# A segment's attention scores as one product over 128 key columns, in attention followed by two feed-forward layers

## The chip, the cores and the metric

One core of one Trainium2 chip runs the whole program. The time is device microseconds of one execution; smaller is better.

## The reference

Three layers in a row, on 4 batches of 544 tokens (32 global, 512 local) and 512 features:

```python
# attention, 8 heads of 64, window 32, scale 1/8
s_g  = scale * q_g @ concat(k_g, k_l).T           # a global query sees all 544 keys
out_g = sm(s_g) @ concat(v_g, v_l)
s_ll = where(abs(i - j) <= 32, scale * q_l @ k_l.T, -1e9)
s_lg = scale * q_l @ k_g.T                        # a local query: its window and the 32 globals
out_l = sm(concat(s_lg, s_ll)) @ concat(v_g, v_l)
x = concat(out_g, out_l)                          # rows of tokens, 512 wide
# feed forward, 512 -> 2048 -> 512
x = (relu(x @ w_in) ** 2) @ w_out
# routed experts: tokens with x @ w_skip > 0 go to one of 8 experts, the others pass
out = x + gate * (relu(x @ w1[e]) @ w2[e])
```

`sm` is the softmax over the last axis. All inputs are float32 values, those of w_in and w_out lie 8 bytes apart and are rebuilt on the chip.

## The kernel before

**Tiles and segments.** The 512 local queries of a batch are 4 tiles of 128, so there are 16 tiles t (batch t // 4, place tt = t % 4 in it). A tile has 4 segments of 32 queries, and each segment sees 96 local keys (a window of three blocks of 32, moved inward at the ends of the sequence) and 32 global keys. The scores of a tile are two PSUM banks `sc` of 128 queries x 4 heads x 128 columns: columns 0 to 95 are the window, 96 to 127 the global keys.

**Scores (`attention`, L413).** `kT[b]` holds the keys of a batch, transposed: 128 partitions (two heads of 64) x 4 pairs of heads x 544 columns, the 512 local keys first and the 32 global ones behind. For a pair of heads the loop writes first the windows of the 4 segments for both heads, then the global columns: 16 products for a pair, 64 for a tile. Each uses 64 rows and 32 columns of TensorE (PE):

```python
for p in range(NPAIR):
    for globals_ in (False, True):
        for i in range(NQ):
            w0 = window(tt, i)
            keys, cols = (slice(SL, S), slice(WIN, P)) if globals_ else (slice(w0, w0 + WIN), slice(0, WIN))
            for g in range(2):
                rows = slice(D * g, D * (g + 1))
                nc.tensor.matmul(scs[g][SEG*i:SEG*(i+1), p, cols], lhsT=q[rows, p, SEG*i:SEG*(i+1)], rhs=kT[b][rows, p, keys], ...)
```

**The rest of a tile.** VectorE (DVE) adds the mask (L426, three masks: first tile of a batch, middle, last), takes the maximum (L430) and scales it (L431). ScalarE (ACT) computes the exps (L433). PE transposes them (L442), ACT or DVE copies them out (L444), and PE multiplies with the values (L451, 32 products into `po`). The value rows of a window stand on 128 partitions in the order of the score columns: rows 0 to 95 the window (L369, L377), rows 96 to 127 the global values (L370, L380). Tiles 0 and 1 use seven places that nothing else uses (`st_v`), the later ones six places in turn (`vr`).

**Keys.** `prep_globals` (L316 to L324) and `prep_k` (L326 to L331) transpose keys on PE into the two-buffered PSUM tag "tr" and copy them to `kT[b]` with ACT: L320 (the globals, 128 columns) and L331 (512 columns, four times for a batch).

**Global queries (`attention_global`).** L485: four products over 512 keys (`gsa`) and four over 32 (`gsb`) for each half of the heads, eight such blocks in all.

**Feed forward and experts.** While the attention of a tile runs, PE works through the feed-forward products of the tiles before it: L697 and L723 at the start, where weights still come in, L700 to L702 and L725 to L727 later. Each chunk of weights is loaded by SP (L209), rebuilt by ACT (L219) and DVE (L223, L227, L233). The activation of the hidden layer runs on ACT (L704, L743) and DVE (L741). Experts follow from some 480 us on.

**Order.** The order of all this is written by hand in strings of letters (SEQ for the first five tiles, EVEN, ODD, TAIL), which a driver turns into calls. Each engine does its instructions in program order, and waits at each for what it needs. SP issues nearly all loads, in order.

Of the kernel before, what the change touches and what calls it, by code (L numbers as in the profile page):

```python
# [8 lines left out]
F32 = mybir.dt.float32  # L9
# [45 lines left out]
def attention_ffn_routed_experts(  # L55
# [73 lines left out]

    masks = {}  # L130
    for kind in range(3):
        m = const.tile([P, P], F32, name=f"mask{kind}")
        nc.gpsimd.memset(m, 0.0)
        for i in range(NQ):
            shift = 0
            if kind == 0 and i == 0:
                shift = SEG
            if kind == 2 and i == NQ - 1:
                shift = -SEG
            seg = m[SEG * i:SEG * (i + 1), 0:WIN]  # L140
            nc.gpsimd.affine_select(
                out=seg, in_=seg, compare_op=ALU.is_ge, fill=NEG,
                base=shift, pattern=[[1, WIN]], channel_multiplier=-1,
            )
            nc.gpsimd.affine_select(
                out=seg, in_=seg, compare_op=ALU.is_ge, fill=NEG,
                base=2 * SEG - shift, pattern=[[-1, WIN]], channel_multiplier=1,
            )
        masks[kind] = m
# [195 lines left out]
    def window(tt, i):  # L345
        return min(max(tt * P + i * SEG - SEG, 0), SL - WIN)

    vin, vgl = {}, {}
    windows, opening, opening_places = [], [], []
# [3 lines left out]
    def load_v(t, part):  # L353
        if t >= NLT:
            return
        b, tt = divmod(t, TPB)
        for i in range(2 * part, 2 * part + 2):
            w0 = window(tt, i)
            if i and w0 == window(tt, i - 1):
# [17 lines left out]
            nc.sync.dma_start(heads(windows[k][0:WIN]), v_l[b, :, w0:w0 + WIN, :].rearrange("h s d -> s h d"))  # L377
            if globals_in.get(k) != b:
                globals_in[k] = b
                nc.sync.dma_start(heads(windows[k][WIN:P]), v_g[b].rearrange("h s d -> s h d"))  # L380
            assert all(w is not windows[k] for w in vin.values())
            vin[t, i] = windows[k]
# [9 lines left out]
    def attention(t, S_TAG, O_TAG):  # L392
        b, tt = divmod(t, TPB)
        q = qT[t // 2][:, :, (t % 2) * P:(t % 2 + 1) * P]
        mask = masks[0 if tt == 0 else 2 if tt == TPB - 1 else 1]
# [10 lines left out]
        for p in range(NPAIR):  # L406
            for globals_ in (False, True):
                for i in range(NQ):
                    w0 = window(tt, i)
                    keys, cols = (slice(SL, S), slice(WIN, P)) if globals_ else (slice(w0, w0 + WIN), slice(0, WIN))  # L410
                    for g in range(2):
                        rows = slice(D * g, D * (g + 1))
                        nc.tensor.matmul(  # L413
                            scs[g][SEG * i:SEG * (i + 1), p, cols],
                            lhsT=q[rows, p, SEG * i:SEG * (i + 1)], rhs=kT[b][rows, p, keys],
                            start=True, stop=True,
                        )
# [4 lines left out]
        for g in range(2):  # L422
            if t != 1:
                sms[g] = sb("sm", 2, [P, S], f"sm{t}_{g}")[:, 0:4 * P]
# [53 lines left out]
    def attention_global(b, S_TAG, O_TAG):  # L478
        for g in range(2):
            sa = ps.tile([P, SL], F32, tag=S_TAG, bufs=BANKS[S_TAG], name=f"gsa{b}_{g}")  # L480
            sb_ = pair(f"gsb{b}_{g}")[:, 0, 0:SG]
            for o, c, n in ((sa, 0, SL), (sb_, SL, SG)):
                for hh in range(4):
                    p, r = divmod(4 * g + hh, 2)
                    nc.tensor.matmul(  # L485
                        o[SG * hh:SG * (hh + 1), :],
                        lhsT=qgT[b][D * r:D * (r + 1), p, :], rhs=kT[b][D * r:D * (r + 1), p, c:c + n],
                        start=True, stop=True,
                    )
# [5 lines left out]
            pg = sb("sm", 2, [P, S], f"pg{b}_{g}")  # L495
            rs = sb("osum", 2, [P, H], f"grs{b}_{g}")
            nc.scalar.activation(pg[:, 0:SL], sa, AF.Exp, bias=mx[:, 3:4], scale=SCALE, accum_out=rs[:, 0:1])
            nc.scalar.activation(pg[:, SL:S], sb_, AF.Exp, bias=mx[:, 3:4], scale=SCALE, accum_out=rs[:, 1:2])
# [5 lines left out]
            for c in range(TPB):  # L504
                nc.tensor.transpose(ptr[:, c, :], pg[:, 0:SL].rearrange("p (k j) -> p j k", j=TPB)[:, c], ident)
# [3 lines left out]
            nc.tensor.transpose(ptr[0:SG, 0, :], pg[:, SL:S], ident)  # L509
# [245 lines left out]
    def ffn_tile(t):  # L755
# [3 lines left out]
        place = sb("kT", 1, [P, NPAIR, S], f"g{t}").rearrange("p a s -> p (a s)")  # L759
# [181 lines left out]
    def wide_tile(e):  # L941
# [4 lines left out]
        def first(f):  # L946
# [8 lines left out]
            gl = sb("sm", 2, [P, S], f"ewgl_{e}_{f}")[:, 0:WIDE].bitcast(F32R)  # L955
# [23 lines left out]
        ys = sb("kT", 1, [P, NPAIR, S], f"ewys_{e}").rearrange("p a s -> p (a s)")[:, 0:KD * WIDE]  # L979
# [42 lines left out]
    def expert_tile(e, j, si):  # L1022
# [4 lines left out]
        hl = sb("kT", 1, [P, NPAIR, S], f"ehl_{name}").rearrange("p a s -> p (a s)")[:, 0:2 * KE * P].bitcast(F32R)  # L1027
# [8 lines left out]
        def first(fb, k0, k1):  # L1036
# [8 lines left out]
            if k1 == KD:  # L1045
                rs[fb] = sb("sm", 2, [P, S], f"er_{name}_{fb}")[:, 0:512]
                nc.scalar.activation(rs[fb], h, AF.Relu)
# [118 lines left out]
    def rest_tile(e, j, in_arm, o):  # L1166
# [13 lines left out]
        r = sb("sm", 2, [P, S], f"er_rest{e}")[:, 0:fw]  # L1180
# [31 lines left out]
    with tc.manual_schedule():  # L1212
# [48 lines left out]
        idle = sb("sm", 2, [P, S], "idle").bitcast(BF16)[:, 0:DM]  # L1261
# [50 lines left out]
        both = sb("kg", 1, [P, 2 * NSLOT], "slots", I32)  # L1312
# [96 lines left out]
        def more(e, j):  # L1409

            if j == UNROLL:
                with tc.For_i(UNROLL, (n_tok[e] + (P - 1)) // P, 1) as it:
                    gi = sb("gi", 2, [P, 1], f"gi{e}", I32)
# [190 lines left out]
```

## Time and profile before

| | |
|---|---|
| median of 3 runs | 708.66 us (707.76 to 709.51) |
| the profiled execution | 710.78 us |
| its span, first to last instruction | 709.1 us, mean granted TensorE clock 0.980 |
| PE busy | 683.5 us, 96% |
| weight loads on PE (PEld) | 574.3 us |
| DVE busy | 396.2 us, 56% |
| ACT busy | 365.5 us, 52% |
| GpSimd (POOL) busy | 163.7 us, 23% |
| DMA | 93.90 MB in 118758 packets, 84789 of them under 512 B |

Times are counted from the span's start. A matmul in float32 leaves two records in the trace for each product. Records overlap on PE, so the sum of their lengths is longer than the time they take; the pace is read from the start of one group to the start of the next. "<-" behind an idle time names what ended it; "issue" means nothing that the profile shows. PEclk is the granted clock, 1.00 being 2.4 GHz and 0.50 being 1.2 GHz.

### The profile page before, as it was taken

Reading aid. Unit: us, or ns where it says so; the run is one execution under the profiler, and the core shown is the slowest. Engines: PE = TensorE matmul, PEld = TensorE weight load, DVE = VectorE, ACT = ScalarE, POOL = GpSimd, SP = SyncE. Lnnn points to the kernel's source line nnn. Section 1 sums busy time; section 2 is a strip of 40 time slices with the busy share of each in tenths; the row PEclk is TensorE's granted clock in tenths of the full one; section 3 lists DMA queues with packets and bytes.
Section 4 is the critical chain, followed back from the end, with each engine's and each line's share of the span. In section 5 each row is a group of like instructions: output and inputs, shape, how many; then the busy total and the mean of one; then the engine's idle time right before and its main releaser. Section 6 shows DMA issues by size and latency. Waiting matters only on the chain. (4 is left out here: it accounts for less than half of the span.)

```text
span 709.1 us, 18592 instructions
## 1 busy us (share of the span) xinstructions
PE 683.5 (96%) x7621; PEld 574.3 (81%) x7621; DVE 396.2 (56%) x1073; ACT 365.5 (52%) x939; POOL 163.7 (23%) x205
## 2 busy tenths in 40 slices
PE   6789999999999999999999999999999999999996
PEld 4566668788888888988898888888887887898875
DVE  1879973873556166165516526544338733915984
ACT  5756557665535545453555545344434514515862
POOL 6000043354211121211221221122220432401311
PEclk8699999999999999999999999999999999999998
DMA  9999744056052501306350120410026588962920
GB/s 273 245 276 245 281 112 106 2 130 125 2 139 61 146 31 36 84 2 146 91 109 32 36 75 2 161 62 1 31 84 201 204 272 285 374 254 77 388 96 21
DMA packets 118758, 93.90 MB, mean 132 GB/s; under 512 B 84789, under 2 KB 91957, under 8 KB 118660
## 3 DMA queue, kind: packets, MB, share of 16 engines
q1 hardware_dynamic: 108352, 71.01, 35.9%
q10 hardware_dynamic: 8292, 15.48, 6.6%
q0 software_dynamic: 2016, 6.09, 2.5%
q8 instruction: 63, 1.03, 0.6%
q14 instruction: 35, 0.29, 0.1%
HBM read 80.31 MB, written 12.66 MB: 131 GB/s over the span
## 5 line engine op out<-in xcount | busy, mean ns | idle before, releaser
L184 POOL TENSOR_TENSOR gl<-g,gh 128x256 fp32r<-128x256 f32 x107 | 79.7, 745 | 302.8 <-ACT gh L183 142.3
L700 PE MATMUL h<-xh,w_in 128*128 128x256 f32 x464 | 134.9, 291 | 0.7 <-ACT xh L183 0.7
L701 PE MATMUL h<-xl,w_in 128*128 128x256 f32 x464 | 129.6, 279 | 0.3 <-DVE xl L184 0.3
L702 PE MATMUL h<-xh,w_in 128*128 128x256 f32 x464 | 129.7, 280 | 0.0
L725 PE MATMUL acc<-w_out,gh 128*128 128x512 f32 x232 | 97.5, 420 | 1.5 <-ACT gh L183 1.5
L727 PE MATMUL acc<-w_out,gl 128*128 128x512 f32 x232 | 91.9, 396 | 0.2
L726 PE MATMUL acc<-w_out,gh 128*128 128x512 f32 x232 | 91.6, 395 | 0.0
L700 PEld LDWEIGHTS h<-xh,w_in 128*128 128x128 f32 x464 | 87.1, 188 | 4.2 <-ACT xh L183 0.9
L704 ACT ACTIVATE g<-h 128x256 f32<-128x256 f32 x128 | 48.9, 382 | 78.9 <-PE h L702 45.0
L701 PEld LDWEIGHTS h<-xl,w_in 128*128 128x128 f32 x464 | 87.2, 188 | 2.6 <-DVE xl L184 0.5
L702 PEld LDWEIGHTS h<-xh,w_in 128*128 128x128 f32 x464 | 87.1, 188 | 0.1
L433 ACT ACTIVATE sm<-sm,mx 128x128 f32<-128x128 f32 x120 | 46.7, 390 | 48.3 <-DVE mx L431 48.3
L741 DVE TENSOR_TENSOR g<-h,g 128x256 f32<-128x256 f32 x53 | 22.2, 420 | 85.5 <-ACT g L704 85.4
L183 ACT CAST gh<-g 128x256 fp32r<-128x256 f32 x116 | 47.2, 407 | 42.4 <-DVE g L741 40.1
L727 PEld LDWEIGHTS acc<-w_out,gl 128*128 128x128 f32 x232 | 43.5, 188 | 11.9 <-POOL gl L184 1.5
L725 PEld LDWEIGHTS acc<-w_out,gh 128*128 128x128 f32 x232 | 43.6, 188 | 8.6 <-ACT gh L183 1.9
L726 PEld LDWEIGHTS acc<-w_out,gh 128*128 128x128 f32 x232 | 43.8, 189 | 5.7
L426 DVE TENSOR_TENSOR sm<-sc,mask 128x512 f32<-128x512 f32 x30 | 20.6, 688 | 24.5 <-PE sc L413 23.7
L255 POOL TENSOR_TENSOR w_in<-st_raw_in,w_in 128x512 fp32r<-128x512 f32 x10 | 13.0, 1309 | 83.1 <-ACT w_in L251 83.1
L743 ACT ACTIVATE g<-g 128x256 f32<-128x256 f32 x63 | 26.2, 416 | 5.1 <-ACT g L704 2.6
L413 PEld LDWEIGHTS sc<-kT,qT 64*32 64x32 f32 x2048 | 25.0, 109 | 4.3 <-issue 3.5
L413 PE MATMUL sc<-kT,qT 64*32 64x96 f32 (+1 forms) x2048 | 27.1, 229 | 0.1
(634 smaller groups left out, 1466.5 us busy)
## 6 DMA issues: line engine op xcount, KB each, us to landing
st_e<-in_moe_w_dram SPq DMA_DIRECT2D x46, 512.0 KB, 5.6
vr<-in_v_l_dram SPq DMA_DIRECT2D x49, 192.0 KB, 4.1
st_raw_in<-in_moe_w_in_dram SPq DMA_DIRECT2D x16, 512.0 KB, 8.1
st_raw_out<-in_moe_w_out_dram SPq DMA_DIRECT2D x16, 512.0 KB, 8.0
st_e<-in_moe_w_dram ACTq DMA_DIRECT2D x12, 512.0 KB, 5.3
x2d<-x ACTq DMA_DIRECT2D x19, 256.5 KB, 3.8
st_gv<-in_v_l_dram SPq DMA_DIRECT2D x8, 512.0 KB, 5.5
out_dram<-x ACTq DMA_DIRECT2D x16, 256.0 KB, 3.7
```

The costliest lines, as they stand in the source:

```text
L183: nc.scalar.copy(hi, src)
L184: (lo_engine or nc.vector).tensor_tensor(out=lo, in0=src, in1=hi.bitcast(F32), op=ALU.subtract)
L413: nc.tensor.matmul(scs[g][SEG * i:SEG * (i + 1), p, cols], lhsT=q[rows, p, SEG * i:SEG * (i + 1)], rhs=kT[b][rows, p, keys], start=True, s ...
L433: nc.scalar.activation(sm[:, hh, :], sm[:, hh, :], AF.Exp, bias=mx[:, hh:hh + 1], scale=SCALE, accum_out=osum[:, 2 * hh + g:2 * hh + g + 1],)
L700: nc.tensor.matmul(h, lhsT=wh, rhs=xh[:, k, :], start=(k == 0), stop=False)
L701: nc.tensor.matmul(h, lhsT=wh, rhs=xl[:, k, :], start=False, stop=False)
L702: nc.tensor.matmul(h, lhsT=wl, rhs=xh[:, k, :], start=False, stop=(k == KD - 1))
L704: nc.scalar.activation(g, h, AF.Relu)
L725: nc.tensor.matmul(acc[z], lhsT=gh[:, c], rhs=wh, start=first_one, stop=False)
L726: nc.tensor.matmul(acc[z], lhsT=gh[:, c], rhs=wl, start=False, stop=False)
L727: nc.tensor.matmul(acc[z], lhsT=gl[:, c], rhs=wh, start=False, stop=last_one)
L743: nc.scalar.activation(square, g, AF.Square)
```

## The change

The keys of a batch are laid out so that every window has the global keys beside it. `kT[b]` gets 21 blocks of 32 columns: the 16 blocks of local keys, with a copy of the 32 global keys behind each group of three (five copies). Any three local blocks in a row and the copy between or behind them are then 128 columns that lie together, and a segment's scores are one product of 128 columns: 32 products for a tile. In the middle of the order of columns (and of value rows) the globals stand at 96, 64 or 32 by the window's place modulo 3 (`globals_at`).

- Keys: `prep_globals` copies the globals to five places at once, `prep_k` copies 480 columns and then 32. For batch 0 the copy of the globals and that of the last 32 columns are on DVE, else on ACT.
- Masks: one for each tt, four instead of three, in bfloat16, of 32x32 pieces.
- Values: a window whose globals stand within it is loaded in two DMAs. Of the seven windows of tiles 0 and 1 only the first gets its global values by DMA; GpSimd copies them into the other six (L399 of the changed kernel).
- `attention_global`: the product over 512 keys becomes one over five runs of 96 and one over 32.
- Some tiles get other sizes or other places for that (not shown): `kT` is larger, `sm` smaller, the expert lists lie in the masks' tile.

```diff
+    BLOCKS = SL // SEG
+    KEYS = (BLOCKS + (BLOCKS - 1) // 3) * SEG
+    def place(n):
+        return (n + n // 3) * SEG
+    def first_block(tt, i):
+        return min(max(tt * NQ + i - 1, 0), BLOCKS - 3)
+    def globals_at(w):
+        return (3 - w % 3) * SEG
...
     def prep_globals(b):
-        kT[b] = sb("kT", 1, [P, NPAIR, S], f"kT{b}")
+        kT[b] = sb("kT", 1, [P, NPAIR, KEYS], f"kT{b}")
         tr = pair(f"kgtr{b}")
         transposes(tr, kin[b, "g"][:, 0:DM], SG)
-        nc.scalar.copy(kT[b][:, :, SL:S], tr[:, :, 0:SG])
+        put = nc.vector.tensor_copy if b == 0 else nc.scalar.copy
+        put(
+            kT[b][:, :, 0:KEYS - SEG].rearrange("p a (g c) -> p a g c", c=P)[:, :, :, WIN:P],
+            tr[:, :, 0:SG].unsqueeze(2).to_broadcast([P, NPAIR, KEYS // P, SG]),
+        )
...
-        nc.scalar.copy(kT[b][:, p, 0:SL].rearrange("p (q j) -> p j q", j=TPB), tr)
+        q = WIN * (KEYS // P) // TPB
+        nc.scalar.copy(
+            kT[b][:, p, 0:KEYS - SEG].rearrange("p (g q j) -> p j g q", j=TPB, q=P // TPB)[:, :, :, 0:WIN // TPB],
+            tr[:, :, 0:q].rearrange("p j (g q) -> p j g q", q=WIN // TPB),
+        )
+        put = nc.vector.tensor_copy if b == 0 else nc.scalar.copy
+        put(kT[b][:, p, KEYS - SEG:KEYS].rearrange("p (q j) -> p j q", j=TPB), tr[:, :, q:P])
...
+    def load_window(o, b, w):
+        at = globals_at(w)
+        for row, n, key in ((0, at, w * SEG), (at + SG, WIN - at, w * SEG + at)):
+            if n:
+                nc.sync.dma_start(heads(o[row:row + n]), v_l[b, :, key:key + n, :].rearrange("h s d -> s h d"))
...
-                nc.sync.dma_start(heads(w[0:WIN]), v_l[b, :, w0:w0 + WIN, :].rearrange("h s d -> s h d"))
-                nc.sync.dma_start(heads(w[WIN:P]), v_g[b].rearrange("h s d -> s h d"))
+                if first_globals:
+                    nc.gpsimd.tensor_copy(w[at:at + SG], first_globals[0])
+                else:
+                    first_globals.append(w[at:at + SG])
+                    nc.sync.dma_start(heads(w[at:at + SG]), v_g[b].rearrange("h s d -> s h d"))
+                load_window(w, b, w0)
...
-            for globals_ in (False, True):
-                for i in range(NQ):
-                    w0 = window(tt, i)
-                    keys, cols = (slice(SL, S), slice(WIN, P)) if globals_ else (slice(w0, w0 + WIN), slice(0, WIN))
-                    for g in range(2):
-                        rows = slice(D * g, D * (g + 1))
-                        nc.tensor.matmul(
-                            scs[g][SEG * i:SEG * (i + 1), p, cols],
-                            lhsT=q[rows, p, SEG * i:SEG * (i + 1)], rhs=kT[b][rows, p, keys],
-                            start=True, stop=True,
-                        )
+            for i in range(NQ):
+                k0 = place(first_block(tt, i))
+                for g in range(2):
+                    rows = slice(D * g, D * (g + 1))
+                    nc.tensor.matmul(
+                        scs[g][SEG * i:SEG * (i + 1), p, :],
+                        lhsT=q[rows, p, SEG * i:SEG * (i + 1)], rhs=kT[b][rows, p, k0:k0 + P],
+                        start=True, stop=True,
+                    )
...
-            for o, c, n in ((sa, 0, SL), (sb_, SL, SG)):
+            most = KEYS - SEG
+            threes = sa[:, 0:SL - SEG].rearrange("p (g c) -> p g c", c=WIN)
+            for o, c in (
+                (threes, slice(0, most)), (sa[:, SL - SEG:SL], slice(most, KEYS)), (sb_, slice(WIN, P)),
+            ):
                 for hh in range(4):
                     p, r = divmod(4 * g + hh, 2)
+                    keys = kT[b][D * r:D * (r + 1), p, c]
+                    if o is threes:
+                        keys = keys.rearrange("p (g c) -> p g c", c=P)[:, :, 0:WIN]
```

PE's order at the scores of the first tile, the first of its four pairs of heads before the change (`sc` and `kT` as above, `qT` the queries):

```order
L413 MATMUL sc_0_273<-kT_198,qT_241 32x96
L413 MATMUL sc_1_274<-kT_198,qT_241 32x96
...
L413 MATMUL sc_0_273<-kT_198,qT_241 32x96
L413 MATMUL sc_1_274<-kT_198,qT_241 32x96
L413 MATMUL sc_0_273<-kT_198,qT_241 32x32
L413 MATMUL sc_1_274<-kT_198,qT_241 32x32
...
L413 MATMUL sc_0_273<-kT_198,qT_241 32x32
L413 MATMUL sc_1_274<-kT_198,qT_241 32x32
```

and the same pair after it (L444 is the line of the product in the changed kernel):

```order
L348 MATMUL ktr_3_280<-ident,st_k_1_207 128x128 x4
L444 MATMUL sc_0_296<-kT_217,qT_263 32x128
L444 MATMUL sc_1_297<-kT_217,qT_263 32x128
L444 MATMUL sc_0_296<-kT_217,qT_263 32x128
...
L444 MATMUL sc_1_297<-kT_217,qT_263 32x128
```

Eight products of 96 columns and eight of 32 became eight of 128; the order of everything else on PE is the same but for the four more products of each global block.

DVE's order at the start, before the change (`st_q` queries, `st_raw_in` raw weights, `sm` masked scores):

```order
L1262 MEMSET idle 128x256
L310 COPY st_q_213<-st_q_in 128x1024
L223 TENSOR_SCALAR st_raw_in_0_256<-st_raw_in_0_256 128x512
L426 TENSOR_TENSOR sm_0_339<-sc_0_273,mask_75 128x512
L430 TENSOR_REDUCE mx_0_341<-sm_0_339 128x4
```

and after it:

```order
L1301 MEMSET idle 128x256
L335 COPY kT_217<-kgtr_218 128x4x5x32
L324 COPY st_q_232<-st_q_in 128x1024
L355 COPY kT_217<-ktr_0_236 128x4x8
L355 COPY kT_217<-ktr_2_243 128x4x8
L355 COPY kT_217<-ktr_1_256 128x4x8
L355 COPY kT_217<-ktr_3_280 128x4x8
L237 TENSOR_SCALAR st_raw_in_0_278<-st_raw_in_0_278 128x512
L457 TENSOR_TENSOR sm_0_330<-sc_0_296,masks_slots 128x512
```

Five copies into `kT` moved in ahead of the first rebuild of weights, one ahead of the copy of queries and four behind it.

## Rows read from the trace of the kernel before

**Rows 1.** The page, part 1 and the instruction queue of part 3

```profile
PE 683.5 (96%) x7621; PEld 574.3 (81%) x7621; DVE 396.2 (56%) x1073; ACT 365.5 (52%) x939; POOL 163.7 (23%) x205
...
q8 instruction: 63, 1.03, 0.6%
```

**Rows 2.** Stretches (us; busy us of each engine, granted clock, DMA share, GB/s)

```profile
18.60:32.00 13.40, 9.97 (x210) 7.09 (x211) 11.62 (x26) 10.38 (x40) 0.00 (x0) 0.50 1.06 253
...
41.60:44.70 3.10, 0.27 (x3) 0.01 (x2) 3.03 (x7) 1.47 (x5) 0.00 (x0) 1.00 0.76 169
44.70:49.20 4.50, 4.50 (x13) 2.49 (x14) 2.29 (x5) 3.54 (x12) 0.00 (x0) 0.63 0.82 284
...
60.00:80.00 20.00, 20.00 (x86) 12.93 (x86) 18.48 (x35) 11.88 (x31) 0.00 (x0) 1.00 1.00 317
...
100.00:480.00 380.00, 377.27 (x4973) 330.83 (x4974) 192.39 (x624) 200.32 (x602) 92.47 (x111) 1.00 0.31 75
```

**Rows 3.** Timeline of PE, a tile's scores (start us, us, line, count)

```profile
119.08 1.62 PE L413 MATMUL sc<-kT,qT 64*32 64x96 f32 x128
120.63 0.50 PE L725 MATMUL acc<-w_out,gh 128*128 128x512 f32 x1
```

**Rows 4.** Timeline of PE, 44 to 52 us

```profile
44.70 0.49 PE L697 MATMUL h<-st_x,st_raw_in 128*128 128x256 f32 x1 [2.83 <-issue]
45.02 0.60 PE L442 MATMUL ptr<-ident,sm 128*128 128x128 f32 x4
45.46 3.21 PE L723 MATMUL acc<-st_raw_out,gh 128*128 128x512 f32 x4
...
49.32 1.90 PE L697 MATMUL h<-st_x,st_raw_in 128*128 128x256 f32 x8
51.14 1.62 PE L413 MATMUL sc<-kT,qT 64*32 64x96 f32 x128
```

**Rows 5.** DMA queues from 41.8 to 43.3 us (packets, MB, share)

```profile
q8 instruction: 1, 0.02, 5.8%
```

**Rows 6.** Timeline of PE, a tile's value products

```profile
163.71 1.10 PE L451 MATMUL po<-vr,pT 128*32 128x64 f32 x64
164.74 0.66 PE L280 MATMUL xtr<-ident,xt 128*128 128x128 f32 x4
```

**Rows 7.** Timeline of PE, products of an expert on 32-column tiles

```profile
599.57 3.35 PE L1194 MATMUL y_rest_a<-st_e,eg_rest_a 128*32 128x128 f32 x110
...
603.40 0.50 PE L1042 MATMUL eh_a<-e0h,xp 128*128 128x512 f32 x1
```

**Rows 8.** Timeline of DVE, 43 to 53 us

```profile
43.81 0.17 DVE L431 TENSOR_SCALAR mx<-mx 128x4 f32<-128x4 f32 x1
...
47.72 0.69 DVE L227 SCALAR_TENSOR_TENSOR st_raw_in<-st_raw_in 128x512 int32<-128x512 int32 x1 [2.21 <-ACT st_raw_in L219]
...
52.93 0.69 DVE L426 TENSOR_TENSOR sm<-sc,mask 128x512 f32<-128x512 f32 x1 [1.71 <-PE sc L413]
```

**Rows 9.** The page, part 5, the exps (busy us, mean ns)

```profile
L433 ACT ACTIVATE sm<-sm,mx 128x128 f32<-128x128 f32 x120 | 46.7, 390 | 48.3 <-DVE mx L431 48.3
```

**Rows 10.** Timeline of ACT at the start

```profile
7.62 0.27 ACT L320 COPY kT<-kgtr 128x128 f32<-128x128 f32 x1
```

**Rows 11.** Timeline of DVE at the start

```profile
9.53 0.69 DVE L310 COPY st_q<-st_q_in 128x1024 f32<-128x1024 f32 x1 [8.13 <-DMA st_q_in<-in_q_l_dram]
...
16.50 0.69 DVE L426 TENSOR_TENSOR sm<-sc,mask 128x512 f32<-128x512 f32 x1 [2.49 <-PE sc L413]
```

**Rows 12.** Instructions of L141, the masks (ns min/median/max, first and last start us)

```profile
L141 POOL TENSOR_SCALAR_AFFINE_SELECT mask<-mask x12: 257/260/267, 1.5 to 8.7; 32x96 f32<-32x96 f32 x12
```

**Rows 13.** Waits of PE, 18.6 to 52 us (us in total, times, longest)

```profile
PE po L451 <- DMA st_v<-in_v_g_dram: 0.8, 2, 0.5
```

**Rows 14.** Timeline of PE, a block of global scores

```profile
193.59 1.06 PE L485 MATMUL gsa<-kT,qgT 64*32 64x512 f32 x8
194.47 0.24 PE L485 MATMUL gsb<-kT,qgT 64*32 64x32 f32 x8
```

More of the change, by code (lines that the diff above doesn't have):

```diff
@@ L128, in attention_ffn_routed_experts, with make_mask @@
     make_identity(nc, ident)
+    BLOCKS = SL // SEG
[6 more added lines that the diff above has]
+        return (3 - w % 3) * SEG
     masks = {}
-    for kind in range(3):
-        m = const.tile([P, P], F32, name=f"mask{kind}")
+    mask_place = const.tile([P, 2 * NSLOT], I32, name="masks_slots")
+    def make_mask(tt):
+        m = mask_place.bitcast(BF16)[:, tt * P:(tt + 1) * P]
         nc.gpsimd.memset(m, 0.0)
         for i in range(NQ):
[L135 to L143, printed above, removed]
-            )
[L145 to L149, printed above, removed]
+            w = first_block(tt, i)
+            for n in range(3):
+                away = w + n - (tt * NQ + i)
+                seg = m[SEG * i:SEG * (i + 1), place(w + n) - place(w):place(w + n) - place(w) + SEG]
+                if abs(away) > 1:
+                    nc.gpsimd.memset(seg, NEG)
+                elif away:
+                    nc.gpsimd.affine_select(
+                        out=seg, in_=seg, compare_op=ALU.is_ge, fill=NEG,
+                        base=0, pattern=[[-away, SEG]], channel_multiplier=away,
+                    )
+        masks[tt] = m
+    for tt in range(TPB):
+        make_mask(tt)
     iota_s = const.tile([P, NSLOT], F32, name="iota_s")
@@ L343, in prep_q @@
                 nc.scalar.copy(qT[j][:, 2 * z + a, :].rearrange("p (q i) -> p i q", i=2), tr[:, a])
-    def window(tt, i):
-        return min(max(tt * P + i * SEG - SEG, 0), SL - WIN)
     vin, vgl = {}, {}
-    windows, opening, opening_places = [], [], []
+    windows, opening, opening_places, first_globals = [], [], [], []
+    def load_window(o, b, w):
[3 more added lines that the diff above has]
+                nc.sync.dma_start(heads(o[row:row + n]), v_l[b, :, key:key + n, :].rearrange("h s d -> s h d"))
     loaded = [0]
@@ L357, in load_v @@
         for i in range(2 * part, 2 * part + 2):
-            w0 = window(tt, i)
-            if i and w0 == window(tt, i - 1):
+            w0 = first_block(tt, i)
+            at = globals_at(w0)
+            if i and w0 == first_block(tt, i - 1):
                 vin[t, i] = vin[t, i - 1]
@@ L376, in load_v @@
             loaded[0] += 1
[L377 to L380, printed above, removed]
+            load_window(windows[k], b, w0)
+            if globals_in.get(k) != (b, at):
+                globals_in[k] = b, at
+                nc.sync.dma_start(heads(windows[k][at:at + SG]), v_g[b].rearrange("h s d -> s h d"))
             assert all(w is not windows[k] for w in vin.values())
@@ L394, in attention @@
         q = qT[t // 2][:, :, (t % 2) * P:(t % 2 + 1) * P]
-        mask = masks[0 if tt == 0 else 2 if tt == TPB - 1 else 1]
+        mask = masks[tt]
         osum = sb("osum", 2, [P, H], f"osum{t}")
@@ L494, in attention_global @@
             nc.vector.tensor_scalar(out=mx[:, 3:4], in0=mx[:, 2:3], scalar1=-SCALE, scalar2=None, op0=ALU.mult)
-            pg = sb("sm", 2, [P, S], f"pg{b}_{g}")
+            pg = sb("sm", 2, [P, SL], f"pg{b}_{g}")
+            pgg = sb("xg", 1, [P, 2, D], f"pgg{b}_{g}")[:, 0, 0:SG]
             rs = sb("osum", 2, [P, H], f"grs{b}_{g}")
-            nc.scalar.activation(pg[:, 0:SL], sa, AF.Exp, bias=mx[:, 3:4], scale=SCALE, accum_out=rs[:, 0:1])
-            nc.scalar.activation(pg[:, SL:S], sb_, AF.Exp, bias=mx[:, 3:4], scale=SCALE, accum_out=rs[:, 1:2])
+            nc.scalar.activation(pg, sa, AF.Exp, bias=mx[:, 3:4], scale=SCALE, accum_out=rs[:, 0:1])
+            nc.scalar.activation(pgg, sb_, AF.Exp, bias=mx[:, 3:4], scale=SCALE, accum_out=rs[:, 1:2])
             yield
@@ L504, in attention_global @@
             for c in range(TPB):
-                nc.tensor.transpose(ptr[:, c, :], pg[:, 0:SL].rearrange("p (k j) -> p j k", j=TPB)[:, c], ident)
+                nc.tensor.transpose(ptr[:, c, :], pg.rearrange("p (k j) -> p j k", j=TPB)[:, c], ident)
             pT = sb("pT", 2, [P, 4, P], f"gpT{b}_{g}")
@@ L508, in attention_global @@
             ptr = pair(f"gptrg{b}_{g}")
-            nc.tensor.transpose(ptr[0:SG, 0, :], pg[:, SL:S], ident)
+            nc.tensor.transpose(ptr[0:SG, 0, :], pgg, ident)
             pTg = sb("pTg", 1, [SG, P], f"gpTg{b}_{g}")
@@ L758, in ffn_tile @@
         acc = ps.tile([P, DM], F32, tag="x2", bufs=2, name=f"acc{t}")
-        place = sb("kT", 1, [P, NPAIR, S], f"g{t}").rearrange("p a s -> p (a s)")
+        place = sb("kT", 1, [P, NPAIR, KEYS], f"g{t}").rearrange("p a s -> p (a s)")
         gs = []
@@ L1179, in rest_tile @@
                 )
-        r = sb("sm", 2, [P, S], f"er_rest{e}")[:, 0:fw]
+        r = sb("sm", 2, [P, SL], f"er_rest{e}")[:, 0:fw]
         nc.scalar.activation(r, h, AF.Relu)
@@ L1310, in attention_ffn_routed_experts @@
                     emit(what)
-        both = sb("kg", 1, [P, 2 * NSLOT], "slots", I32)
+        both = mask_place
         gidx, sidx = both[:, 0:NSLOT], both[:, NSLOT:2 * NSLOT]
```

21 lines of the change are left out of this document (10 added, 11 removed).

## The prediction

> **What bounds the kernel now.** Read first the page's busy times and instruction queue [rows 1]: TensorE (PE) works 683.5 of 709.1 us, so time is won where PE gets less to do or waits less. Then the stretches [rows 2]. From 100 us on PE is busy 377.27 of 380 us, and VectorE (DVE) half the time: there each microsecond taken from PE comes off the end. Before that it does not. From 41.6 to 44.7 us PE does 0.27 us of work, the stretch behind it runs at a granted clock of 0.63, and from 60 to 80 us DVE is busy 18.48 of 20 us with the rebuilding of weights that PE will want: PE can be early there only by as much as DVE is.
>
> Then the work that the change touches. A tile's scores are one solid block [rows 3]: from 119.08 to the next line at 120.63 us, 1.55 us for 128 matmul records (64 products of two records each). 13 of the 16 blocks take 1.55 to 1.56 us; 12 of the 16 lie after 100 us. In those 1.55 us go 128 records and 128 weight loads, 12.1 ns for a record.
>
> Then the hole at 41.9 us [rows 4]: the h product (L697) at 44.70 us waits 2.83 us for "issue", so for nothing that the profile names. In 41.8 to 43.3 us one packet of the instruction queue moved [rows 5], while the DMA engines were busy with weights (a share of 0.76 over the hole [rows 2]). 63 packets for 2 x 7621 records on PE is 242 records for a packet. I read the hole as PE having run out of fetched instructions behind a queue that the weights' DMAs held up. The weak point of this reading: no row joins that packet to PE.
>
> **The change, part by part; the sum is made against the profiled execution (span 709.1, 710.78 us), which stands 2.1 us above the runs' median 708.66, and the differences are taken off the median.**
>
> *Scores, 64 products to 32.* No row shows a product of 64 rows by 32 columns with 128 columns streamed. The nearest:
> - Value products (L451), also on 32-column tiles and 64 records [rows 6]: 163.71 to 164.74 us, 1.03 us, 16.1 ns a record for 64 columns at full height (four tiles). The new block is 64 records with 128 columns, on twice as many tiles (two heads in the two halves of the rows): the same columns for each tile in turn. I take 1.03 us, so 0.52 less for a block.
> - Lower bound: the present rate holds, 64 x 12.1 ns = 0.78 us, 0.77 less.
> - Upper bound: 128-column records on four tiles [rows 7]: 128 records (110 in the row shown, 18 in three small groups behind it) from 599.57 to 603.40 us, 3.83 us or 29.9 ns each; 64 of them make 1.91 us, 0.36 more than now. That needs the two row halves to take turns. The present block speaks against it: it streams the same 64 x 128 columns and is done in 1.55 us. With halves that overlap, 0.96 us.
> The 12 late blocks: 12 x 0.52 = **-6.2 us**. The first four lie where others set the pace (below).
>
> *The hole.* The change takes 128 matmul and weight-load records out of each of the first blocks (64 of either kind a tile), so by 41 us some 384 fewer are fetched, 1.6 packets. The edge of a packet that fell at the seventh L697 falls later, in the work around the next block, and its packet is asked for earlier against PE's need. I take the hole as gone. What then is late next? The second exps of tile 2: their maximum ends at 43.98 us on DVE [rows 8]; four exps of 0.39 us [rows 9] end at 45.6; transposes 0.44 (45.02 to 45.46) and products 1.82 us (49.32 to 51.14) [rows 4] bring tile 3's scores to 47.8 us instead of 51.14. PE gains 3.3 us of the 2.83 plus the slow clock behind it (4.5 us at 0.63 in place of 0.99 is 1.6). DVE must follow [rows 8]: its 2.21 us wait for ACT at 47.72 shrinks to 0.7, since ACT's rebase (L219) and the exps ahead of it were queued behind the activation of the h that was held up, and now start some 1.5 us sooner; its 1.71 us wait for the scores at 52.93 goes. Together 3.2 us: **-3.2 us**. The bounds: nothing, if the hole stays, but the 0.5 of a block; and 4.5 if DVE's other waits shrink too.
>
> *The start.* ACT loses the 0.27 us copy of the global keys [rows 10] and a sixteenth of each of four longer copies; DVE takes over one copy of 640 columns and four small ones, which stand around its 0.69 us copy of queries at 9.53 us [rows 11]. A transpose that needs the bank waits for the later of the two engines: between 0.3 gained and 0.3 lost; I take **+0.2 us**. GpSimd: 36 small mask instructions in place of 27, at 0.26 us each [rows 12] 2.3 us more, and six copies of value rows. It does nothing in the stretches of [rows 2] up to 80 us, and DVE first uses a mask at 16.50 us [rows 11], 8 us after the last select of that line began [rows 12]: nothing, unless its copies for tile 0's windows come later than about 22 us.
>
> *The value rows.* Six of seven v_g DMAs go, 0.39 MB in 256-byte packets; at the 253 GB/s of 18.6 to 32 us [rows 2] 1.5 us of DMA time. PE waited 0.8 us for two of them [rows 13], in a stretch where DVE sets the pace: nothing by itself; it is the margin for weights that PE would now want 3 us sooner. 36 of the 56 windows come in two DMAs; in the middle DMA engines have a share of 0.31 [rows 2] and no row waits for them: nothing.
>
> *Global scores.* The four products over 512 keys, 0.88 us from 193.59 to 194.47, become four of 480 and four of 32 [rows 14]. The 32-column group there is 0.24 us long, its end over the next line's start; between 0 and 0.2 more, I take 0.1, for six of eight blocks after 100 us: **+0.6 us**. Each later batch has five more ACT copies of 0.1 to 0.3 us before transposes that wait for ACT: **+0.2 us**.
>
> Sum: -6.2 - 3.2 + 0.2 + 0.6 + 0.2 = **-8.4 us**: 702.4 us for a profiled execution, **700.2 us** for the median.
>
> The Trainium skill (TensorE: Matmul & The Clock Gate, "Part 3: Packing small matmuls") says that a weight load overlaps running matmuls only where its row group differs from theirs. The value products of rows 6 all use the whole height, one row group, and 64 of them still run at 16.1 ns, so loads are not what holds them; the rule by itself speaks for rival C below, with a sum of -6.2 us in place of -8.4.
>
> **The rivals.**
> - **B: the hole stays or reopens elsewhere before 80 us.** For it: no row joins packet and hole; the DMA share is about 1 until 80 us [rows 2], so any other edge of a packet could be late too. Against: the hole is "issue", not a wait for data. Then the lead is 0.5 to 1.3 us instead of 3.2: 708.66 - 8.4 + 2.3 = 702.6 us. The Trainium skill (Runtime: NRT & Kernel Launch, "Instruction fetch mechanics") holds that fetching is hidden by the pace of issue. If that is so here, the hole has another cause which the change would leave. The 2.83 us with an instruction packet inside speak against it, and I leave it in B's chance of 0.18.
> - **C: weight loads come to the front.** A block that streams longer per load frees the next tile later. If a product of both records costs 38 ns rather than 32, the block is 1.22 us and saves 0.33: 12 x 0.33 = 4.0 us in place of 6.2, 702.4 us. For it: the weight loads are as many as the matmuls [rows 1], and halving both leaves each load with a longer stream on its tile. Against: the pace of [rows 6]. Chance 0.08.
> - **D, slower: the two row halves take turns when each streams 128 columns.** A block then takes 1.91 us by rows 7, 0.36 more, 4.3 us for 12 blocks. From 1.75 us up the block eats the 2.4 us of all other parts (12 x 0.20), so D decides from there. With the hole gone it ends at 708.66 + 4.3 - 2.2 = 710.8 us, with the hole left at 708.66 + 4.3 + 0.5 = 713.5 us. Against it is the 1.55 us of the present block for the same columns. Chance 0.05.
>
> **How the numbers follow.** Forecast 0.66, B 0.18, C 0.08, D 0.05, and 0.03 for a new wait at the start (tile 0's value rows from GpSimd, masks) that costs 5 us or more. Low end: blocks at 0.78 us and all else as forecast is 708.66 - 11.4 = 697.2; the hole's upper bound takes another 1: 696.3. High end: B and C together, 704.6, rounded to 704.4. A measurement of this kernel tells a difference of 0.3% (2.1 us) from none. Faster by more needs less than 706.5: forecast, B and C, 0.92, less 0.03 for B and C in their worse halves together: 0.89. Within 0.3%: 0.06, part of D and of the new wait. Slower: 0.05.
>
> **What would show it.** In the profile of the changed kernel: the score block late in the span (about 1.0 us for 64 records; 0.8 or 1.2 or 1.9 say which bound); no "issue" wait above 1 us on PE between 32 and 80 us and tile 3's scores near 48 us; PE and DVE some 3 us early at 97 us; DVE's first mask addition at 16.3 to 16.9 us; the global block 0.1 us longer. A steady block above 1.75 us, or a wait of several microseconds for value windows before 60 us, makes the prediction wrong.

## The result, and the profile after

The changed kernel takes **702.29 us** (median of 6 runs, 701.17 to 703.27) beside 709.09 us for the kernel before: a ratio of 0.9901, 95% interval 0.9874 to 0.9929, so 7.0 us less by the ratio (5.0 to 8.9) and 6.8 by the medians. The forecast was 700.2 us, 8.4 less, in a range of 696.3 to 704.4. The profiled executions stand further apart, 699.5 against 709.1 us of span: the one of before is 1.7 us over its kernel's median now, the one of after 1.1 us under.

The page after, its span, busy times and instruction queue; it answers to [rows 1]:

```profile
span 699.5 us, 16771 instructions
...
PE 675.6 (97%) x6661; PEld 565.1 (81%) x6661; DVE 395.9 (57%) x1078; ACT 365.9 (52%) x950; POOL 165.8 (24%) x220
...
q8 instruction: 56, 0.92, 0.6%
```

960 matmul records and as many weight loads are gone from PE, and with them 7 packets of instructions; 1920 / 256 is 7.5.

The stretches after, in the columns of [rows 2]:

```profile
41.60:44.70 3.10, 2.18 (x9) 1.19 (x8) 3.03 (x7) 3.08 (x13) 0.00 (x0) 1.00 1.01 378
44.70:49.20 4.50, 4.50 (x62) 2.98 (x63) 3.74 (x8) 4.14 (x14) 0.00 (x0) 1.00 1.04 398
...
100.00:470.00 370.00, 367.37 (x4216) 319.91 (x4215) 188.17 (x620) 198.80 (x606) 91.51 (x110) 1.00 0.31 77
```

PE works 2.18 us in the stretch that had held the hole (0.27 before), and the clock behind it stays at 1.00 (0.63 before). The late part is PE's as it was.

Timeline of PE after, the place of [rows 4]:

```profile
42.19 1.40 PE L473 MATMUL ptr<-ident,sm 128*128 128x128 f32 x4
44.38 2.07 PE L762 MATMUL acc<-st_raw_out,gh 128*128 128x512 f32 x4 [0.79 <-ACT gh L782]
46.29 0.60 PE L473 MATMUL ptr<-ident,sm 128*128 128x128 f32 x4
46.72 1.90 PE L736 MATMUL h<-st_x,st_raw_in 128*128 128x256 f32 x8
48.55 1.16 PE L444 MATMUL sc<-kT,qT 64*32 64x128 f32 x64
```

No wait of PE for "issue" is left in the whole trace; tile 3's scores begin at 48.55 us (51.14 before; 47.8 forecast).

A late block of scores after, beside [rows 3]:

```profile
115.88 1.16 PE L444 MATMUL sc<-kT,qT 64*32 64x128 f32 x64
116.97 0.50 PE L764 MATMUL acc<-w_out,gh 128*128 128x512 f32 x1
```

1.09 us in place of 1.55. Timeline of DVE at the start and in the first 50 us after, beside [rows 8, 11]:

```profile
16.97 0.22 DVE L355 COPY kT<-ktr 128x32 f32<-128x32 f32 x1 [3.14 <-ACT kT L350]
17.08 0.42 DVE L237 TENSOR_SCALAR st_raw_in<-st_raw_in 128x512 int32<-128x512 int32 x1
17.70 0.69 DVE L457 TENSOR_TENSOR sm<-sc,masks_slots 128x512 f32<-128x512 f32 x1 [0.20 <-PE sc L444]
...
46.87 0.69 DVE L241 SCALAR_TENSOR_TENSOR st_raw_in<-st_raw_in 128x512 int32<-128x512 int32 x1 [0.76 <-ACT st_raw_in L233]
...
50.41 0.67 DVE L457 TENSOR_TENSOR sm<-sc,masks_slots 128x512 f32<-128x512 f32 x1
```

The first mask addition is 1.2 us later than before (17.70 for 16.50), so in these two traces the start cost a whole microsecond more than the 0.2 forecast. The 2.21 us wait for ACT has become 0.76 (0.7 forecast), and the 1.71 us wait for tile 3's scores is gone: its mask addition, at 52.93 before, runs at 50.41.

### The profile page after: what moved, and what is told of

It reads as the page before. It is cut to its first block, busy times and chain, and to the rows that moved or that the text cites. A ratio compares the mean times of both kernels' runs of the same rounds, so it can differ in the third digit from the quotient of the medians.

```text
span 699.5 us, 16771 instructions
## 1 busy us (share of the span) xinstructions
PE 675.6 (97%) x6661; PEld 565.1 (81%) x6661; DVE 395.9 (57%) x1078; ACT 365.9 (52%) x950; POOL 165.8 (24%) x220
## 5 line engine op out<-in xcount | busy, mean ns | idle before, releaser
L457 DVE TENSOR_TENSOR sm<-sc,masks_slots 128x512 f32<-128x512 f32 x30 | 20.6, 685 | 15.4 <-PE sc L444 14.4
L762 PE MATMUL acc<-st_raw_out,gh 128*128 128x512 f32 x48 | 23.9, 618 | 0.8 <-ACT gh L782 0.8
L473 PE MATMUL ptr<-ident,sm 128*128 128x128 f32 x120 | 20.3, 286 | 2.6 <-ACT sm L464 2.4
```

The lines of the kernel that those rows point to most:

```text
L762: nc.tensor.matmul(acc[z], lhsT=gh[:, c], rhs=w, start=first_one, stop=last_one)
```

## The experiments

All times are medians; ratios are to the kernel before in the same batch, with 95% intervals. The kernel before itself stood at 708.6 to 709.2 us in them. The changed kernel was not run again, so a difference from its 702.29 us is one between batches, with some 2 us of uncertainty either way. "Instruction n" counts PE's matmuls, weight loads and semaphore instructions in the order in which they start in the trace; a stop "ahead of n" is given from the start of the instruction before it to the start of n itself.

**1. Two products again, everything else changed.**

```diff
-            for i in range(NQ):
+            for c0, c1 in ((0, WIN), (WIN, P)):
+                for i in range(NQ):
...
-                        scs[g][SEG * i:SEG * (i + 1), p, :], ... rhs=kT[b][rows, p, k0:k0 + P],
+                        scs[g][SEG * i:SEG * (i + 1), p, c0:c1], ... rhs=kT[b][rows, p, k0 + c0:k0 + c1],
```

> The changed kernel with each score product of 128 columns split into one of 96 and one of 32 columns, in the order of before; layout of keys, masks, value copies and start as changed. PE gets 128 records a tile more, so as many as before. Theory 1 (PE ran out of fetched instructions: it holds packets of 256, asks for the next at each edge, and stops where 256 instructions go by faster than a packet takes to arrive while the DMA engines are full): the hole is back, an 'issue' wait of 2.5 to 3.5 us at a feed-forward product near 42 us, tile 3's scores at 51 us or later, the late score blocks at 1.55 us; 710 to 711 us. Rival (the hole went because 0.39 MB of value rows no longer load at the start): no such wait, the late blocks at 1.55 us, so 5.6 us over the changed kernel's 702.3, about 708 us.

Measured 709.84 us, ratio 1.0001 (0.9986 to 1.0016): without the merged products nothing of the gain is left. The timeline of PE in this kernel:

```profile
38.56 3.51 PE L737 MATMUL h<-st_x,st_raw_in 128*128 128x256 f32 x15
43.75 0.38 PE L737 MATMUL h<-st_x,st_raw_in 128*128 128x256 f32 x1 [1.68 <-issue]
...
48.47 1.51 PE L445 MATMUL sc<-kT,qT 64*32 64x96 f32 x107
50.31 0.42 PE L445 MATMUL sc<-kT,qT 64*32 64x96 f32 x21 [0.34 <-issue]
```

The hole is back at the same product, but 1.68 us long where 2.5 to 3.5 was expected, and the total lies just under the 710 expected. The counts say more than the lengths. In the kernel before PE stops ahead of instructions 449 (21.08 to 21.57 us) and 1217 (41.48 to 44.69). Here it stops ahead of 449, 1217 and 1473. 1217 - 449 is 3 x 256, 1473 - 1217 is 256. PE stops at packet edges. (A fourth stop, far behind these, is told in experiment 6.)

**2. The hole moved to a place named beforehand.**

```diff
+            for _ in range(43):
+                nc.tensor.matmul(o[:, 0:32], lhsT=idle[:, 0:P], rhs=idle[:, 0:32], start=True, stop=True)
```

> The changed kernel with 43 tiny products (86 PE instructions, 32 columns of zeros) more among the warming products before 7 us, where PE is idle anyway. Theory 1 puts the edges of the packets 86 instructions earlier in the program: one falls at the start of tile 3's scores (48.4 us) and the next at the end of its value products (50.6 us), 256 instructions later. So PE should stop there for 'issue', 2.5 to 5.5 us long at about 50.7 us, at a feed-forward product (second layer) of the first tile, and the whole should take 704 to 707 us. Rival (the hole had nothing to do with instructions): no wait above 0.5 us there, 702.3 us as the changed kernel.

Measured 710.43 us, ratio 1.0014 (0.9990 to 1.0039): 43 products of zeros, done while PE was idle anyway, take the whole gain away. Timeline of PE:

```profile
48.35 1.16 PE L444 MATMUL sc<-kT,qT 64*32 64x128 f32 x64
49.44 1.18 PE L482 MATMUL po<-vr,pT 128*32 128x64 f32 x62
53.23 0.30 PE L482 MATMUL po<-vr,pT 128*32 128x64 f32 x2 [2.62 <-issue]
```

The stop came ahead of instruction 1217 once more, which now is one of the last value products of tile 3, four instructions short of the place expected, with 2.62 us inside the bounds. But the total was expected at 704 to 707 us, and 2.6 us is not 8. PE is 2.6 to 2.7 us behind the changed kernel from 70 to 460 us; the rest goes in the experts, which no theory had named. Waits of PE after 60 us (us in total, times, longest), and stretches with the columns of [rows 2]:

```profile
PE ewh_a L990 <- issue: 3.5, 1, 3.5
```

```profile
597.00:612.90 15.90, 15.90 (x99) 13.04 (x92) 14.99 (x27) 10.19 (x17) 6.26 (x3) 1.00 1.05 372
612.90:617.00 4.10, 0.58 (x4) 0.32 (x3) 0.97 (x2) 0.44 (x1) 1.02 (x1) 0.78 1.05 385
617.00:627.00 10.00, 10.00 (x54) 10.00 (x55) 0.98 (x2) 0.88 (x2) 0.00 (x0) 0.75 0.94 350
```

A second stop for "issue", of 3.5 us, again at a DMA share of 1.05 (expert weights), and behind it 10 us at a clock of 0.75. In the changed kernel PE is busy for all 26.0 us from 594 to 620 us, at a clock of 1.00. There are branches ahead of it, so the count by 256 can't be carried there: that this stop is at a packet's edge too is likely, not shown. In favour of it, a packet of the instruction queue runs inside the stop, from 614.42 to 615.54 us, and PE's next product follows 1.25 us later.

**3. Global values by DMA again.**

```diff
-                if first_globals:
-                    nc.gpsimd.tensor_copy(w[at:at + SG], first_globals[0])
...
+                nc.sync.dma_start(heads(w[at:at + SG]), v_g[b].rearrange("h s d -> s h d"))
```

> The changed kernel with the global value rows of all seven windows of tiles 0 and 1 loaded by DMA again, none copied on GpSimd. Prediction's view: 0.39 MB more at the start lie in a stretch that the rebuilding of weights on VectorE sets; PE waits up to 0.8 us more for values near 30 us, which is hidden; 702.3 us, within 0.7. Rival: the DMA queue is what sets the first 80 us, and 1.5 us more of it show at the end: 703.5 us or more, and a wait for instructions comes back.

Measured 702.07 us, ratio 0.9892 (0.9869 to 0.9916), as the changed kernel. In it the value copies are worth nothing that these runs can tell.

**4. Global queries first** (`keys_in` and `queries_in` are the two halves of `prep_globals`).

```diff
+        for part in (queries_in, keys_in) if b == 0 else (keys_in, queries_in):
+            part()
```

> The changed kernel with the global queries of batch 0 transposed before the global keys, so that the first transpose of keys takes the PSUM bank that ScalarE's short copy frees and not the one behind VectorE's 0.82 us copy. Theory: the start of the changed kernel is 1.2 us late (first mask addition at 17.70 us in place of 16.50), because PE waits for VectorE's copies out of the transposes' banks; here 0.6 to 0.9 us of it come back and, as VectorE sets the pace up to 100 us, stay to the end: 701.5 us. Rival: later waits (weights still landing) take it back: 702.3 us.

Measured 702.60 us, ratio 0.9901 (0.9878 to 0.9925): PE is 0.76 us ahead of the changed kernel at 19 us, and 0.28 ahead from 154 us on. The start came back as the theory said, the end did not follow; a 0.3 us gain is below what these runs can tell. One trace alone would not show the start either, since it varies: the six traces of experiments with the start as changed have their first mask addition between 16.81 and 18.31 us (16.94 here). Counted from the first transpose of the globals, it comes 9.5 to 10.6 us later in them and in the changed kernel, 9.3 us later in both traces of the kernel before, and 9.2 us later here.

**5. The kernel before with shifted edges.**

```diff
-WARM = 8
+WARM = 132
...
-                nc.tensor.matmul(o, lhsT=idle[:, 0:P], rhs=idle, start=True, stop=True)
+                nc.tensor.matmul(o[:, 0:32], lhsT=idle[:, 0:P], rhs=idle[:, 0:32], start=True, stop=True)
```

> The kernel before the change with nothing but other warming products: 132 of 32 columns in place of 8 of 512, so 248 PE instructions more, which puts every edge of a packet of 256 instructions 8 instructions later in the program (248 is 256 less 8) at about the same length of warming. Theory 1: the stop moves from behind the last products of h (the 1217th instruction) to the transposes or second-layer products of 42 to 45 us, where PE has waited long enough for the packet to arrive; the stop of 2.83 us shrinks under 1.5 us, and the kernel before gets 2 to 4 us faster without any change of its work: 705 to 707 us. Rival (the stop belongs to that h product or to its data): it stays at 41.4 us, 709 us.

Measured 710.09 us, ratio 1.0015 (0.9999 to 1.0032): a miss. Timeline of PE, and its waits from 18.6 to 60 us:

```profile
41.90 3.73 PE L697 MATMUL h<-st_x,st_raw_in 128*128 128x256 f32 x16
45.47 0.49 PE L442 MATMUL ptr<-ident,sm 128*128 128x128 f32 x3
46.97 0.33 PE L442 MATMUL ptr<-ident,sm 128*128 128x128 f32 x1 [1.01 <-ACT g L704]
```

```profile
PE po L451 <- DMA st_v<-in_v_g_dram: 1.4, 2, 1.2
```

The h products run through: the stop did move, as the theory says, to the transposes ahead of instruction 1473 (1217 and 256), 45.69 to 46.97 us, where the profile puts 1.01 us of it down to ACT. But the global value rows came later than in [rows 13], 1.4 us of waits for 0.8, and the scores of tile 2, at 36.80 us before, began at 39.99. PE was slower there too: from 32.0 to 41.6 us its granted clock is 0.53 in this trace, 0.99 in that of the kernel before. What the smaller stop gave had been lost ahead of it, and as the edit changed the warming along with the edges, this run doesn't tell the price of the stop.

**6 and 7. Two products in the late tiles alone, or in the early ones alone.** The second kernel has `t < 4` in the line below.

```diff
-            for i in range(NQ):
+            for c0, c1 in ((0, WIN), (WIN, P)) if t >= 4 else ((0, P),):
+                for i in range(NQ):
...
```

> The changed kernel with the score products of tiles 4 to 15 alone split into 96 and 32 columns again (12 x 128 records, six packets exactly). Theory: 12 x 0.465 us, the difference of the late score blocks, and no stop for instructions: 702.3 + 5.6 = 707.9 us. Rival (the late blocks cost less at the end than on PE, since others wait there): under 706 us.

Measured 708.23 us, ratio 0.9989 (0.9975 to 1.0002), 5.9 us over the changed kernel (6.2 by the ratios). Eleven of its twelve blocks after 100 us take 1.56 us; that of 371.78 us takes 2.12. Waits of PE (us in total, times, longest):

```profile
PE pr L687 <- PE sc L445: 0.5, 1, 0.5
```

The profile puts this wait down to PE itself, but it is a stop too, where none was expected: it lies ahead of instruction 9153 (373.33 to 373.90 us), which is 449 and 34 x 256, and a packet of the instruction queue ends at 372.58 us. The DMA engines have a share of 0.00 from 371.5 to 374.0 us. All 256 instructions from edge to edge are one block of scores here and pass in 1.55 us; the packet, started at 371.29, doesn't come in time. Experiment 1 has the same stop ahead of 9665 (375.00 to 375.56 us). The late blocks are worth what their difference says, 12 x 0.466 = 5.6 us; the stop adds about half a microsecond.

> The changed kernel with the score products of tiles 0 to 3 alone split into 96 and 32 columns again (4 x 128 records, two packets exactly). Theory 1: the stop for instructions at the 1217th is back, 1.5 to 3 us long, and costs 2 to 3 us at the end beside the late blocks, which stay at 1.09 us: 704.3 to 705.3 us. Rival (a stop in the first 60 us is hidden by the rebuilding of weights): 702.3 us.

Measured 703.51 us, ratio 0.9928 (0.9909 to 0.9948): 1.2 us over the changed kernel, less than expected. By the ratios it is 1.9 us. The stops are ahead of 449 (22.51 to 23.37 us) and 1217 (42.85 to 43.19), so the second is a tenth of the first profile's here, and PE is not idle in it. Up to there this is the program of experiment 1, whose trace has PE idle for 1.68 us at that place: the length of a stop differs from run to run. 5.9 and 1.2 make 7.1, which is what splitting all tiles cost (709.84 - 702.29 = 7.6), within the intervals.

**8. The four segments of one head, then of the other.**

```diff
-            for i in range(NQ):
-                k0 = place(first_block(tt, i))
-                for g in range(2):
-                    rows = slice(D * g, D * (g + 1))
+            for g in range(2):
+                rows = slice(D * g, D * (g + 1))
+                for i in range(NQ):
+                    k0 = place(first_block(tt, i))
```

> The changed kernel with the products of a pair of heads in another order: the four segments of one head (the upper half of the rows), then the four of the other. Theory: eight tiles stream side by side as long as PE gets at products of both halves in turn; with four of one half in a row a half waits, and a block takes between 1.1 and 1.9 us (1.9 if the halves take turns fully): 702.3 to 712 us. Rival (PE looks far enough ahead): 1.09 us, 702.3 us.

Measured 701.84 us, ratio 0.9900 (0.9875 to 0.9924), late blocks 1.09 us: the order of products in a pair of heads doesn't matter. Four of one half in a row don't make the halves take turns.

**9. The value copies alone, in the kernel before.**

```diff
+                if len(opening) > 1:
+                    nc.gpsimd.tensor_copy(w[WIN:P], opening[0][WIN:P])
+                else:
+                    nc.sync.dma_start(heads(w[WIN:P]), v_g[b].rearrange("h s d -> s h d"))
...
-                nc.sync.dma_start(heads(w[WIN:P]), v_g[b].rearrange("h s d -> s h d"))
```

> The kernel before with one part of the change alone: the global value rows of tiles 0 and 1 come once by DMA and are copied by GpSimd for the other six windows. Theory: PE's waits for those rows (0.8 us) go, the stop for instructions stays at the 1217th instruction; within 1 us of the kernel before, 708 to 709.5 us. Rival (0.39 MB less at the start also bring the instruction packets sooner, so that the stop goes): 706 us or less.

Measured 707.34 us, ratio 0.9968 (0.9953 to 0.9982): 2.3 us less by the ratio, 1.9 by the medians, which lies between the two expectations. Timeline of PE:

```profile
38.05 3.51 PE L700 MATMUL h<-st_x,st_raw_in 128*128 128x256 f32 x15
42.18 0.49 PE L700 MATMUL h<-st_x,st_raw_in 128*128 128x256 f32 x1 [0.62 <-issue]
42.51 0.60 PE L445 MATMUL ptr<-ident,sm 128*128 128x128 f32 x4
```

The stop is at the same product and ahead of the same instruction 1217, but 0.62 us long. The instruction packet that ends it starts at 39.57 us, where it started at 41.97 before: 2.9 us after PE passed the edge before, at 961, in place of 5.0. Two other pairs of traces that differ in the copies alone go the same way, 1.6 in place of 3.8 us (experiments 10 and 5, behind the edge at 1217) and 2.2 in place of 3.1 (the changed kernel and experiment 3, behind that at 705). With 0.39 MB of small packets less in the DMA queues this packet comes sooner. The one for the stop ahead of 449 doesn't (19.40 us for 18.85), and PE is idle for 0.72 us there.

**10. Shifted edges and value copies together, in the kernel before.**

> The kernel before with shifted packet edges (the warming products of the earlier experiment) and the value copies together. There the stop had shrunk, but PE waited 1.4 us for global value rows by DMA at 33 to 35 us and VectorE fell 2.2 us behind. Theory: without that wait the smaller stop shows at the end, 2 us or more below the value copies alone: 705.5 to 707.5 us. Rival (a stop in the first 60 us is worth little at the end in most runs, VectorE being what sets that stretch): 708 to 710 us.

Measured 707.71 us, ratio 0.9978 (0.9964 to 0.9992), between the two ranges and no better than the copies alone, so the theory's further 2 us are not there. With the stop at 0.6 us there was little left to shift away.

**11. A second profile of the kernel before.**

> The kernel before, unchanged, for a second profile. Theory 1: the stop is again at the 1217th PE instruction, but its length is how late that packet came, so it differs from the first profile's 2.83 us (1 to 4 us), and a shorter stop goes with a shorter execution than the 710.78 us of the first, by up to as much as the stop is shorter and the clock behind it higher.

The execution took 710.64 us, and the timeline of PE shows nearly the same stop:

```profile
44.55 0.49 PE L697 MATMUL h<-st_x,st_raw_in 128*128 128x256 f32 x1 [2.60 <-issue]
```

2.60 us for 2.83, ahead of instruction 1217 again (41.57 to 44.55 us); 0.14 us less in time for 0.23 us less of stop. Both profiled executions lie 1.4 us or more over the median of their kernel, so they don't tell how long the stop is in a middling run.

## Why the prediction was right, point by point

- **Scores, 64 products to 32: right, the term a little large.** 0.46 us less for a block where 0.52 was taken: 12 x 0.46 = 5.6 for 6.2 us, and experiment 6 finds 5.9 at the end with half a microsecond of a stop in it. The value products were the right price for the pace: their records start 14.0 ns apart, those of the new block 14.1. The 0.06 us between 1.03 and 1.09 are its longer end, 0.20 in place of 0.15 us from the last record to the next line. That pace is half of the one on four tiles [rows 7] (28.5 ns from start to start; the 29.9 has the end in it), as it would be if eight tiles stream side by side. The records of the old block stream 64 columns on average and start 11.3 ns apart, not 7: that is why half as many records of twice the length save time. Rivals C (1.22 us) and D (1.91 us) are out. The weight loads are as many as the matmuls in the new block as well, and it holds the same pace as the value products. The rule of the Trainium skill (TensorE: Matmul & The Clock Gate, "Part 3: Packing small matmuls") that a load overlaps only matmuls of another row group would have put loads in front in experiment 8, where four products of one half follow each other, and there the block is the same.
- **The hole: right in place and cause, with half of the cause missing.** PE stops at each 256th instruction if that packet is late: shown by the stops ahead of 449, 1217 and 1473 in kernels where those instructions are scores, h products or value products, and by the stop put at tile 3's values in experiment 2. All thirteen traces of this case agree: up to 480 us PE has 15 waits in them that the profile puts down to "issue" or to PE itself, and every one begins at instruction 449 or a multiple of 256 behind it. Behind each of them PE goes on 1.3 to 1.6 us after the last packet of the instruction queue has ended, which is the row that the prediction missed between packet and hole. How late the packet is depends on the small value packets in the DMA queues, as experiment 9 and the two other pairs beside it show, and differs between runs besides (experiment 7). The prediction set those at "nothing by itself". So either part of the change is enough to shorten the stop: with merged products the copies add nothing (experiment 3), with copies alone PE's idle time at the stop falls from 2.6 to 2.8 us to 0.6, and with the copies in experiments 1 and 7 it is 1.7 and nothing. Where a cause takes two things, 256 instructions going by fast and a packet coming late, taking out one leaves little for the other to give. The Trainium skill (Runtime: NRT & Kernel Launch, "Instruction fetch mechanics") has instructions come in blocks of 256, and the traces agree; its sentence that fetching is hidden does not hold here, by 2.83 us.
- **The price of the hole was taken from the profiled execution and then off the median: the step that the runs bear out least.** The forecast of 8.4 us lies inside 5.0 to 8.9, so they don't refute it. In the profiles the early part comes out as forecast: VectorE is 3.2 us ahead at 100 us (forecast 3.2, less 0.2 for the start), made of 1.2 us lost at the start and 4.4 us won from 40 to 80 us, about the upper bound given (4.5). In the medians it is 7.0 - 5.9 = 1.1 us (0.8 by the ratios), and experiment 7 finds 1.2 (1.9). Two accounts of that are open. One is that the stop is shorter, or hidden, in most runs: both profiles of the kernel before lie 1.4 to 1.7 us over its median, at a mean granted clock of 0.980. Of its 69 runs beside the experiments, 10 have a clock of 0.982 or less, with a median of 710.5 us; the other 59 have 708.8. That points to it, but no view shows a run that wasn't profiled. The other is that the rest of the change (the start, the new order of keys, windows in two DMAs, the global products) costs more than was taken. The copies alone gain 2.3 us (1.3 to 3.3, experiment 9), and experiment 1, which has all of the change but the merged products, is 2.3 us slower than that, though its stops are longer too (3.0 us of idle time in its trace, for 1.3). No run takes these parts one by one.
- **The start: mis-sized, 1.2 us for 0.2 in the two profiles.** The copy of 640 columns on VectorE held the first transpose of keys until 8.97 us (7.94 before), and transposes at 11.41 and 13.89 us waited for VectorE's small copies, 0.5 us each. Counted from the first transpose of the globals, the traces with this start lose 0.2 to 1.3 us, 1.0 in the changed kernel's. Experiment 4 took it away, 0.76 us against that trace, and nothing of it shows at the end, where less than 2 us can't be told.
- **Global scores and later copies: mis-sized.** The global block takes 189.19 to 190.08 us for its first two parts, 0.89 for 0.88: nothing where 0.6 was taken in sum, nor do PE's waits show the 0.2 for copies. From tile 4's scores to tile 15's the changed kernel wins 4.87 us (334.83 to 329.96), where eleven blocks at 0.466 make 5.13: some 0.3 us is left of the 0.8. This error and the 0.6 on the blocks nearly cancel, which is luck.
- **Rival B** (the hole stays or reopens) did not happen, but experiment 2 shows how near it was: 86 instructions more ahead of it, and both a hole at 50 us and one at 613 us open.
- **Slips that don't move the forecast.** By its own terms B and C together end at 704.8 us (708.66 - 8.4 + 2.3 + 2.2), not 704.6. In D the other parts stand at 2.4 and at 2.2 us, and 2.2 is their sum. And 14 of the 16 blocks before take 1.55 to 1.56 us, not 13.

## What to carry to other kernels

Count instructions as well as columns: products that stream longer take fewer packets of instructions, and a stretch where 256 PE instructions pass in a few microseconds (4.6 ahead of the hole, 2.1 in experiment 2) while the DMA queues are full is where PE stops for "issue". Where they passed in 1.55 us, it stopped for half a microsecond with the queues empty (experiment 6). Such a stop stays at the same count when the program is edited ahead of it, so any edit can move it into or out of a dense place, which is worth up to 8 us here and looks like an effect of the edit; count from the trace before believing one. And take a term of a profiled execution off a median only where every run has it.

## What was not expected of the hardware

A stop costs more than its length, through the clock: 10 us at a granted clock of 0.75 follow the 3.5 us at 613 us (experiment 2), and 4.5 us at 0.63 followed the 2.83 us of the kernel before [rows 2]. Six short DMAs of value rows, 0.39 MB in all, held an instruction packet back by some 2 us (it starts at 41.97 us with them, at 39.57 without, in one trace each). And eight 64-row tiles of 32 columns each stream side by side at 14.1 ns a record of 128 columns, in either order of the heads.
